# Attention weights exchanged between partition blocks before, instead of after, VectorE's block transposes

## The chip, the cores and the metric

The kernel runs on one core of one Trainium2 chip. A core has a TensorE (PE, with its weight loads listed apart as PEld), a VectorE (DVE), a ScalarE (ACT), a GpSimd (POOL) and a SyncE (SP) that here only issues DMAs; sixteen DMA engines move the data. [...] The metric is the device time of one execution, in microseconds; the median of three executions is given.

## The reference, cut to what matters

```python
# q, k, v: (8, 8, 576, 64) float32; tau a scalar
scores = scale * q @ k^T
thresh = max(scores) - tau
scores = where(scores >= thresh, scores, -1e9)
attn = softmax(scores)                    # exp, sum + 1e-9, divide
x = (attn @ v) as (4608, 512)
h = x @ w_in                              # (4608, 1024), weights float64
e = exp(h - max(h)); solu = h * e / (sum(e) + 1e-9)
ln = (solu - mean) / sqrt(var + 1e-6) * g_ln
out = ln @ w_out                          # (4608, 512)
```

The attention weights `attn` come out with the queries on the partitions. The product with `v` needs the keys on the partitions, so each block of weights has to be transposed.

## The kernel before, in words

**Rounds.** The attention is cut into 144 slots of two heads by 128 queries, 18 for each of the eight batches. A loop written out by hand (from L746) gives one round to each slot and puts the work of several slots and of the feed-forward part into every round, in a fixed order. In round s:

- PE makes the scores of slot s for two heads into two PSUM tiles `s_ps` (`scores`, L396). In some rounds it first turns q and k of a later batch (L269).
- DVE takes the negated row maxima (`maxes`, L412). ACT makes the threshold and a ramp, which is the first write of the weights `w` (`ramp`, L423 and L427), and then the exponentials in place with their sums `sm` (`exps`, L437). The ramp is the last reader of the score columns of `s_ps`; only then can PE write the scores of slot s+1.
- POOL normalises slot s-1: two small instructions make the reciprocal of the sums (L444, L445), and two of 128x576 multiply `w` in place (L447).
- DVE transposes the weights of slot s-1 in blocks of 32x32 (`blocks`, L459) into a tile `T` that serves two slots, a unit. After the second slot of a unit, SP issues four DMAs (L470) that take each 32 partitions of `T` and lay their two halves of columns out over 64 partitions of `wT`: 288 KB each, with runs of 4608 bytes.
- PE multiplies `wT` with `v` (`attend`, L495), for a unit whose second slot is s at round s+3 at the earliest.

**Feed-forward.** A tile of 128 tokens goes through rounds in a repeated pattern of four. In two rounds PE makes h (`ff_h`, L548), and in these two it also does one `attend` each. In the next two it makes the output of the tile before (`ff_o`, L650). I call them H1, H2, O1 and O2; H1 and H2 follow O2. In H2, DVE transposes the V of the tile before (`ff_turn`, L638) and takes the maximum of h (`ff_max`, L561), which ACT's exponential of h in round O1 needs (`ff_exp`, L570). In O1, DVE multiplies (`ff_mul`, L576) and POOL makes a reciprocal (`ff_sum`, L581). In O2, DVE makes mean and variance (L591, L592) and POOL five small results from them (`ff_stats`, L595 to L602). In H1, ACT and DVE normalise (L612, L617), and SP issues four DMAs that exchange halves of u with V (`ff_swap`, L628); the output of a tile is stored there too (L677). In the H1 round, a POOL memset (`fence`, L104) stands between PE's two parts of h.

**Order in a round.** The order in the program's loop is: loads of the next batch on SP, scores, maxes, ramps and exps, `normalise`, jobs of the middle (`ff_stats`; `ff_norm2` and `ff_swap`), PE's feed-forward and `attend`, `blocks`, late jobs (`ff_turn`, `ff_max`, `ff_mul`, `ff_sum`, `ff_store`). In the first 16 rounds each round ends with the conversion of one piece of the float64 weights on DVE and ACT (L221 to L247) and the DMAs of a later piece (L205, L210, L256).

**Buffers.** `w` has four buffers of one head each (two rounds), `T` and `wT` two each. All of the kernel's DMAs from round 0 on are issued by SP.

Of the kernel before, what the change touches and what calls it, by code (L numbers as in the profile page):

```python
# [8 lines left out]
F32 = mybir.dt.float32  # L9
# [4 lines left out]
ALU = mybir.AluOpType  # L14
AX = mybir.AxisListType
PSUM = bass.MemoryType.PSUM
P = 128
# [3 lines left out]
def kernel(  # L21
# [27 lines left out]
    nc = tc.nc  # L49
    B, H, S, D = q.shape  # L50
# [6 lines left out]
    NB = S // 32  # L57
    SCALE = 0.125
    ROWS = (slice(0, 64), slice(64, P))
# [4 lines left out]
    work = ctx.enter_context(tc.tile_pool(name="work", bufs=2))  # L64
# [21 lines left out]
    NK = S // 64  # L86
# [4 lines left out]
    units = {}  # L91
# [171 lines left out]
    def turn(spare, x, lhsT_of):  # L263

        o = spare["base"] + 64 * x
        to = slice(o, o + 64)
        for r in range(2):
            for y in range(2):
                nc.tensor.matmul(  # L269
                    out=spare[r][ROWS[y], to], lhsT=lhsT_of(r, y), rhs=ident[ROWS[r], ROWS[r]],  # L270
                    start=True, stop=True,
                )

    def seen(spare, r, x, n):
        o = spare["base"] + 64 * x
        return spare[r][:, o : o + 64 * n].rearrange("p (t k) -> p t k", t=n)

    def source(i):
        b, hp = divmod(i, NP)
        return halves[b, hp // 2], 2 * (hp % 2)  # L280

    def pair(i):
        if i not in pairs:
            pairs[i] = dict(
                qT=heads.tile([P, SM], F32, tag="qT", name="qT"),
                kT=heads.tile([P, S], F32, tag="kT", name="kT"),
                qe=heads.tile([P, ST], F32, tag="qe", name="qe"),
            )
        return pairs[i]
# [23 lines left out]
    def k_parts(i):  # L313

        return pair(i)["kT"].rearrange("p (c m k) -> p m c k", c=2, m=NK)

    def k_item(i, ts=slice(0, 4)):
        src, h0 = source(i)
        to = k_parts(i)
        n = ts.stop - ts.start  # L320

        def make(spare, x):
            for t in range(n):
                turn(spare, x + t, lambda r, y: src["k"][ROWS[r], h0 + y, ts.start + t])

        def keep(spare, x, r):
            (nc.vector.tensor_copy if r and not spare.get("eased") else nc.scalar.copy)(
                out=to[:, 4 * r + ts.start : 4 * r + ts.stop],
                in_=seen(spare, r, x, n).rearrange("p t (k c) -> p t c k", c=2),
            )  # L330

        return n, make, keep

    def e_item(i):
        src, h0 = source(i)
        last = k_parts(i)[:, NK - 1]

        def make(spare, x):
            turn(spare, x, lambda r, y: ends[i // NP][ROWS[r], 2 * (i % NP) + y])

        def keep(spare, x, r):
            if r == 0:
                nc.scalar.activation(
                    out=pair(i)["qe"], in_=seen(spare, 0, x, 1)[:, 0], func=AF.Copy, scale=scl
                )
            else:
                (nc.scalar.copy if spare.get("eased") else nc.vector.tensor_copy)(
                    out=last, in_=seen(spare, 1, x, 1)[:, 0].rearrange("p (k c) -> p c k", c=2)
                )

        return 1, make, keep
# [21 lines left out]
    live = {}  # L373
# [45 lines left out]
    def ramp(s, x):  # L419
        d = live[s]  # L420
        ps = d["ps"][x]
        nth = small.tile([P, 1], F32, tag="nth", name="nth")
        nc.scalar.activation(  # L423
            out=nth, in_=d["nth"][x], func=AF.Identity, bias=tau_t, scale=1.0
        )
        w = work.tile([P, S], F32, tag="w", bufs=4, name="w")
        nc.scalar.activation(  # L427
            out=w, in_=ps[:, 0:S], func=AF.Prelu, bias=nth, scale=1.0,
            alpha=1.0e30,
        )  # L430
        d.setdefault("w", []).append(w)

    def exps(s):
        d = live[s]
        d["sm"] = sm = small.tile([P, 2], F32, tag="sm", name="sm")
        for x, w in enumerate(d["w"]):
            nc.scalar.activation(  # L437
                out=w, in_=w, func=AF.Exp, bias=ntau, scale=1.0, accum_out=sm[:, x : x + 1]
            )

    def normalise(s):
        d = live[s]
        sm = d["sm"]
        nc.gpsimd.tensor_scalar(out=sm, in0=sm, scalar1=1e-9, scalar2=None, op0=ALU.add)  # L444
        nc.gpsimd.tensor_tensor(out=sm, in0=sm, in1=mone, op=ALU.pow)  # L445
        for x, w in enumerate(d["w"]):
            nc.gpsimd.tensor_scalar(  # L447
                out=w, in0=w, scalar1=sm[:, x : x + 1], scalar2=1.0, op0=ALU.mult, op1=ALU.mult
            )

    def blocks(s):
        b, kind, hp, r = slots[s]
        key = (b, kind, hp)
        if r == 0:
            units[key] = dict(T=work.tile([P, NB, 2, 2, 32], F32, tag="T", name="T"))
        u = units[key]
        T = u["T"]
        for h, w in enumerate(live.pop(s)["w"]):
            nc.vector.transpose(out=T[:, :, r, h, :], in_=w)  # L459
        if r == 0:  # L460
            return


        T = T.rearrange("p (c m) r h x -> p c (m r h x)", c=2)
        u["wT"] = wT = work.tile([P, 2, NK, 2, 2, 32], F32, tag="wT", bufs=2, name="wT")
        to = wT.rearrange("p g m r h x -> p g (m r h x)")
        for g in range(2):
            for half in range(2):
                of = 64 * half + 32 * g
                nc.sync.dma_start(out=to[ROWS[half], g], in_=T[of : of + 32])  # L470

# [234 lines left out]
    for b in range(1, B):  # L708
        r = PER * (b - 1)
# [7 lines left out]
    with tc.manual_schedule():  # L717
# [3 lines left out]
        for x in range(3):  # L721
# [4 lines left out]
            out=g_rows.rearrange("c (r g x) -> c r g x", r=2, g=2),  # L726
            in_=g_ln.rearrange("(g c r x) -> c r g x", g=2, r=2, x=32),
# [10 lines left out]
        rnd = 0  # L738
# [7 lines left out]
        while True:  # L746
# [29 lines left out]
            if more:  # L776
                room = SPARE
                if busy and quarter > 1 and preps and rnd + 4 < first_slot(preps[0][3]):
                    room = 0
                while preps and preps[0][0] <= rnd and preps[0][1] <= room:  # L780
                    _, n, make, _ = preps.pop(0)
                    items.append(make())
                    room -= n
                scores(rnd, items)
                maxes(rnd)
                ramp(rnd, 0)
                keeps(rnd, 0)
                keeps(rnd, 1)
                ramp(rnd, 1)
                exps(rnd)  # L790
            if rnd in whole:
                whole_pair(whole[rnd])
            if rnd - 1 in live:
                normalise(rnd - 1)
            for job in middle.pop(rnd, []):
                job()
            due = bool(pv_due) and pv_due[0][0] <= rnd
            step = None
            if quarter < 2 and cur is not None:
# [43 lines left out]
            if attending is not None:  # L843
# [4 lines left out]
                    ready.append((rnd + 1, [(b // 2,)]))  # L848
                elif kind < 2 and hp == NP - 1:
                    ready.append((rnd + 1, [(b, kind, 0), (b, kind, 1)]))  # L850
            if rnd - 1 in live:
                blocks(rnd - 1)
            for job in late.pop(rnd, []):
                job()
            if rnd == 2:
# [1 line left out]
            if rnd in pieces:  # L857
                x = pieces[rnd]
# [42 lines left out]
```

## Time and profile before

| | |
|---|---|
| median of three executions | 927.46 us (927.3 to 929.27) |
| the profiled execution | 931.87 us, of which the span from first to last instruction is 930.1 us |
| mean granted TensorE clock | 0.98 |
| busy: PE / DVE / ACT / POOL | 853.2 / 675.7 / 668.7 / 448.8 us |
| DMA queue of SP | 94472 packets, 150.13 MB, 70.0% of sixteen engines |
| `wT<-T` | 288 DMAs of 288 KB, median 5.8 us from issue to landing |
| `V<-u` | 144 DMAs of 64 KB, median 3.7 us from issue to landing |
| L447, the multiplications on POOL | 288 of 128x576, mean 768 ns |
| L459, the block transposes | 288 of 128x576, mean 750 ns |

In the profile's groups, a line gives: program line, engine, operation, tiles, shape and count, then the total and the mean duration, then the idle time just before these instructions and what ended it. A timeline's line gives: start, duration, engine, line, operation, tiles, shape, count, and in brackets the idle time ahead of it with what ended it; neighbouring instructions of one line are merged, so that the duration is that of all of them together. SPq stands for SP's instruction queue, where the duration is that of the issue and not of the transfer.

### The profile page before, as it was taken

The page shows a single profiled execution, that of the slowest core. Times are in us where ns is not written, and L with a number is a line of the kernel's source. Part 1 is how long each engine was busy: PE and PEld are TensorE (multiplying, and loading weights), DVE is VectorE, ACT ScalarE, POOL GpSimd, SP SyncE. Part 2 cuts the span into 40 slices and gives each one's busy share as a digit, 9 for nine tenths or more (in the row PEclk, how much of TensorE's full clock was granted, in tenths as well). Part 3 has the DMA queues.
Part 4 walks back from the last instruction along what each step waited for, and adds up shares of the span by engine and source line. Part 5 has one row for each costly group of instructions (what it writes and reads, how often), then busy time and mean ns, then how long its engine had stood idle before and what let it go on. Part 6 is the DMA issues. An engine that isn't in the chain of part 4 may idle for free. (4 is left out here: it accounts for less than half of the span.)

```text
span 930.1 us, 39744 instructions
## 1 busy us (share of the span) xinstructions
PE 853.2 (92%) x17089; PEld 643.3 (69%) x17089; DVE 675.7 (73%) x1015; ACT 668.7 (72%) x1531; POOL 448.8 (48%) x870
## 2 busy tenths in 40 slices
PE   4548689989999999989999999989998999999997
PEld 3325478857678778866677887767776877777555
DVE  4888977768767877767777777767876777787352
ACT  5767877878777877867777787868877777888121
POOL 1443555536545555545545555545555455655220
PEclk9978799999999999999999999999999999999999
DMA  8898967975879558965879467966889455866422
GB/s 245 195 224 229 223 162 187 229 176 126 182 163 226 128 129 191 238 137 128 189 166 227 108 134 185 230 147 132 189 180 211 114 130 127 185 145 139 96 47 47
DMA packets 95880, 154.63 MB, mean 166 GB/s; under 512 B 27608, under 2 KB 69592, under 8 KB 95704
## 3 DMA queue, kind: packets, MB, share of 16 engines
q1 hardware_dynamic: 94472, 150.13, 70.0%
q8 instruction: 134, 2.20, 1.0%
q10 hardware_dynamic: 1232, 1.97, 0.7%
q14 instruction: 42, 0.34, 0.1%
HBM read 46.14 MB, written 9.44 MB: 60 GB/s over the span
## 5 line engine op out<-in xcount | busy, mean ns | idle before, releaser
L412 DVE TENSOR_REDUCE nm<-s_ps 128x1 f32<-128x576 f32 x288 | 204.6, 752 | 164.5 <-PE s_ps L396 164.1
L650 PE MATMUL o_ps<-w,uT 64*64 64x256 f32 x4608 | 271.6, 378 | 7.5 <-DVE uT L638 4.6
L650 PEld LDWEIGHTS o_ps<-w,uT 64*64 64x64 f32 x4608 | 230.4, 134 | 56.5 <-issue 18.4
L427 ACT ACTIVATE w<-s_ps,nth 128x576 f32<-128x576 f32 x288 | 213.6, 742 | 20.2
L548 PE MATMUL h_ps<-w,xh 64*64 64x512 f32 x1856 | 222.5, 594 | 4.1 <-issue 4.1
L447 POOL TENSOR_SCALAR w<-w,sm 128x576 f32<-128x576 f32 x288 | 217.4, 768 | 14.4
L437 ACT ACTIVATE w<-w,ntau 128x576 f32<-128x576 f32 x288 | 219.1, 764 | 0.0
L459 DVE STREAM_TRANSPOSE T<-w 128x576 f32<-128x576 f32 x288 | 205.9, 750 | 6.1 <-POOL w L447 5.6
L495 PEld LDWEIGHTS pv<-wT,v 64*64 64x64 f32 x5760 | 169.5, 136 | 40.7 <-issue 28.1
L396 PE MATMUL s_ps<-kT,qT 64*64 64x512 f32 (+1 forms) x2048 | 174.8, 422 | 20.6 <-ACT w L427 17.9
L444 POOL TENSOR_SCALAR sm<-sm 128x2 f32<-128x2 f32 x144 | 36.7, 255 | 321.6 <-ACT w L437 318.9
L495 PE MATMUL pv<-wT,v 64*64 64x128 f32 (+1 forms) x5760 | 171.8, 263 | 11.3 <-DMA wT<-T 7.7
L548 PEld LDWEIGHTS h_ps<-w,xh 64*64 64x64 f32 x1856 | 116.0, 135 | 93.8 <-issue 71.0
L423 ACT ACTIVATE nth<-nm,tau_t 128x1 f32<-128x1 f32 x288 | 84.5, 294 | 95.6 <-DVE nm L412 95.2
L445 POOL TENSOR_TENSOR sm<-sm,mone 128x2 f32<-128x2 f32 x144 | 103.6, 719 | 12.0
L396 PEld LDWEIGHTS s_ps<-kT,qT 64*64 64x64 f32 x2048 | 66.0, 138 | 30.6 <-ACT w L427 25.7
L612 ACT ACTIVATE V<-u,nb,rs 128x1024 f32<-128x1024 f32 x36 | 44.6, 1240 | 32.3 <-POOL nb L602 32.3
L638 DVE STREAM_TRANSPOSE uT<-V 128x1024 f32<-128x1024 f32 x36 | 44.0, 1222 | 20.1 <-DMA V<-u 19.9
L517 ACT COPY xh<-pv 128x256 f32<-128x256 f32 x64 | 23.5, 367 | 44.7 <-PE pv L495 44.4
L437 ACT ACTIVATION_READ_ACCUMULATOR w<-w,ntau 128x1 f32 x288 | 54.7, 190 | 0.0
L570 ACT ACTIVATE u<-h_ps,hm 128x1024 f32<-128x1024 f32 x36 | 40.3, 1119 | 20.0 <-DVE hm L561 14.6
L561 DVE TENSOR_REDUCE hm<-h_ps 128x1 f32<-128x1024 f32 x36 | 43.0, 1194 | 11.6 <-PE h_ps L539 6.2
(74 smaller groups left out, 633.2 us busy)
## 6 DMA issues: line engine op xcount, KB each, us to landing
wT<-T SPq DMA_DIRECT2D x288, 288.0 KB, 5.8
V<-u SPq DMA_DIRECT2D x144, 64.0 KB, 3.7
out_dram<-ob SPq DMA_DIRECT2D x72, 128.0 KB, 2.8
v<-in_v_dram SPq DMA_DIRECT2D x16, 512.0 KB, 8.0
v<-in_v_dram SPq DMA_DIRECT2D x32, 256.0 KB, 7.4
q<-in_q_dram SPq DMA_DIRECT2D x15, 512.0 KB, 5.7
k<-in_k_dram SPq DMA_DIRECT2D x15, 512.0 KB, 7.7
raw<-in_moe_w_out_dram SPq DMA_DIRECT2D x32, 128.0 KB, 5.3
```

The costliest lines, as they stand in the source:

```text
L396: nc.tensor.matmul(out=ps[h][ROWS[y], ks], lhsT=lhsT, rhs=d["kT"][ROWS[h], ks], start=True, stop=True,)
L412: nc.vector.tensor_reduce(out=nm, in_=ps[:, 0:S], axis=AX.X, op=ALU.max, negate=True)
L423: nc.scalar.activation(out=nth, in_=d["nth"][x], func=AF.Identity, bias=tau_t, scale=1.0)
L427: nc.scalar.activation(out=w, in_=ps[:, 0:S], func=AF.Prelu, bias=nth, scale=1.0, alpha=1.0e30,)
L437: nc.scalar.activation(out=w, in_=w, func=AF.Exp, bias=ntau, scale=1.0, accum_out=sm[:, x : x + 1])
L445: nc.gpsimd.tensor_tensor(out=sm, in0=sm, in1=mone, op=ALU.pow)
L447: nc.gpsimd.tensor_scalar(out=w, in0=w, scalar1=sm[:, x : x + 1], scalar2=1.0, op0=ALU.mult, op1=ALU.mult)
L459: nc.vector.transpose(out=T[:, :, r, h, :], in_=w)
L495: nc.tensor.matmul(out=to, lhsT=d["v"][ROWS[u], h0 + h, m ^ 4 * u if m < 8 else m], rhs=rhs, start=m == 0, stop=m == NK - 1,)
L548: mm = nc.tensor.matmul(out=h[ROWS[y], f], lhsT=x[ROWS[r], c, ROWS[y]], rhs=w1[ROWS[r], c, f], start=part == 0 and c == 0, stop=part == 1 ...
L612: nc.scalar.activation(out=V, in_=u, func=AF.Identity, bias=nb, scale=rs)
L650: nc.tensor.matmul(out=d["o"][ROWS[z], 512 * r : 512 * r + 256], lhsT=d["uT"][ROWS[r], m].rearrange("p y x -> p (y x)"), rhs=w2[ROWS[r], m ...
```

## The change

The weights' columns of each head are exchanged between partition blocks before the transposes. `normalise` now writes a second tile `wx` instead of `w`, with the same product. A new step `spread`, after the jobs of the middle of the same round, lets POOL also multiply `w` in place, and then lets SP issue four DMAs for each slot: each takes half of the columns of both heads of 32 partitions from `w` into 32 other partitions of `wx`, 72 KB in runs of 1152 bytes. So half of each row of `wx` is POOL's, and half comes by DMA. `blocks` transposes `wx` straight into `wT`, two rounds after the slot instead of one; `T` and its DMAs are gone. `w` and `wx` have three buffers of two heads each. The columns of k are laid out in another order to fit (L329 and L348, source of a copy read in runs instead of every second element). The earliest round of `attend` is unchanged.

```diff
-                in_=seen(spare, r, x, n).rearrange("p t (k c) -> p t c k", c=2),
+                in_=seen(spare, r, x, n).rearrange("p t (c k) -> p t c k", c=2),
...
-        w = work.tile([P, S], F32, tag="w", bufs=4, name="w")
+        if x == 0:
+            d["w"] = work.tile([P, 2, S], F32, tag="w", bufs=3, name="w")
+        w = d["w"][:, x]
...
-        for x, w in enumerate(d["w"]):
+        d["wx"] = work.tile([P, 2, S], F32, tag="wx", bufs=3, name="wx")
+        times(d["wx"], d)
+
+    def times(to, d):
+        for x in range(2):
             nc.gpsimd.tensor_scalar(
-                out=w, in0=w, scalar1=sm[:, x : x + 1], scalar2=1.0, op0=ALU.mult, op1=ALU.mult
+                out=to[:, x], in0=d["w"][:, x], scalar1=d["sm"][:, x : x + 1], scalar2=1.0,
+                op0=ALU.mult, op1=ALU.mult,
             )
+    def spread(s):
+        d = live[s]
+        w, wx = d["w"], d["wx"]
+        times(w, d)
+        for g in range(2):
+            for half in range(2):
+                here, there = 64 * half + 32 * g, 64 * half + 32 * (1 - g)
+                nc.sync.dma_start(
+                    out=wx[here : here + 32, :, S // 2 * (1 - g) : S // 2 * (2 - g)],
+                    in_=w[there : there + 32, :, S // 2 * g : S // 2 * (g + 1)],
+                )
 
     def blocks(s):
...
-            units[key] = dict(T=work.tile([P, NB, 2, 2, 32], F32, tag="T", name="T"))
...
-        for g in range(2):
-            for half in range(2):
-                of = 64 * half + 32 * g
-                nc.sync.dma_start(out=to[ROWS[half], g], in_=T[of : of + 32])
+            units[key] = dict(
+                wT=work.tile([P, 2, NK, 2, 2, 32], F32, tag="wT", bufs=2, name="wT")
+            )
+        to = units[key]["wT"].rearrange("p g m r h x -> p (g m) r h x")
+        wx = live.pop(s)["wx"]
+        for h in range(2):
+            nc.vector.transpose(out=to[:, :, r, h, :], in_=wx[:, h])
...
             for job in middle.pop(rnd, []):
                 job()
+            if rnd - 1 in live:
+                spread(rnd - 1)
...
-            if rnd - 1 in live:
-                blocks(rnd - 1)
+            if rnd - 2 in live:
+                blocks(rnd - 2)
```

More of the change, by code (lines that the diff above doesn't have):

```diff
@@ L347, in keep @@
                 (nc.scalar.copy if spare.get("eased") else nc.vector.tensor_copy)(
-                    out=last, in_=seen(spare, 1, x, 1)[:, 0].rearrange("p (k c) -> p c k", c=2)
+                    out=last, in_=seen(spare, 1, x, 1)[:, 0].rearrange("p (c k) -> p c k", c=2)
                 )
@@ L430, in ramp @@
         )
-        d.setdefault("w", []).append(w)
     def exps(s):
@@ L435, in exps @@
         d["sm"] = sm = small.tile([P, 2], F32, tag="sm", name="sm")
-        for x, w in enumerate(d["w"]):
+        for x in range(2):
+            w = d["w"][:, x]
             nc.scalar.activation(
@@ L445, in normalise @@
         nc.gpsimd.tensor_tensor(out=sm, in0=sm, in1=mone, op=ALU.pow)
-        for x, w in enumerate(d["w"]):
+        d["wx"] = work.tile([P, 2, S], F32, tag="wx", bufs=3, name="wx")
+        times(d["wx"], d)
+    def times(to, d):
+        for x in range(2):
             nc.gpsimd.tensor_scalar(
-                out=w, in0=w, scalar1=sm[:, x : x + 1], scalar2=1.0, op0=ALU.mult, op1=ALU.mult
-            )
+                out=to[:, x], in0=d["w"][:, x], scalar1=d["sm"][:, x : x + 1], scalar2=1.0,
+                op0=ALU.mult, op1=ALU.mult,
+            )
+    def spread(s):
[9 more added lines that the diff above has]
+                )
     def blocks(s):
@@ L454, in blocks @@
         if r == 0:
-            units[key] = dict(T=work.tile([P, NB, 2, 2, 32], F32, tag="T", name="T"))
[L456 to L466, printed above, removed]
-        for g in range(2):
-            for half in range(2):
-                of = 64 * half + 32 * g
-                nc.sync.dma_start(out=to[ROWS[half], g], in_=T[of : of + 32])
+            units[key] = dict(
[5 more added lines that the diff above has]
+            nc.vector.transpose(out=to[:, :, r, h, :], in_=wx[:, h])
     def attend(key):
```

## The prediction

> **What bounds the kernel now.** I read the page's busy shares and slices first.
>
> ```profile
> PE 853.2 (92%) x17089; PEld 643.3 (69%) x17089; DVE 675.7 (73%) x1015; ACT 668.7 (72%) x1531; POOL 448.8 (48%) x870
> PE   4548689989999999989999999989998999999997
> DMA  8898967975879558965879467966889455866422
> ```
>
> There are two stages. In the first six slices (140 us) PE is half busy and the DMA engines are full. After that PE is full, so only what makes PE wait can cost time there. The waits show what the change could relieve:
>
> ```profile
> PE pv L495 <- DMA wT<-T: 7.7, 2, 7.3
> DVE T L459 <- POOL w L447: 5.6, 7, 3.3
> ```
>
> PE waited twice for the DMA that goes (7.7 us in all, one of them 7.3 us long, in the first 70 us). The next view is the timeline of one four-round cycle in the full stage: PE, DVE, POOL and ACT around 430 us.
>
> ```profile
> 425.08 1.18 PE L396 MATMUL s_ps<-kT,qT 64*64 64x64 f32 x16
> 426.05 3.66 PE L650 MATMUL o_ps<-w,uT 64*64 64x256 f32 x64
> 429.50 1.18 PE L396 MATMUL s_ps<-kT,qe 64*64 64x64 f32 x16
> ```
> ```profile
> 421.64 1.43 DVE L459 STREAM_TRANSPOSE T<-w 128x576 f32<-128x576 f32 x2
> 422.99 1.20 DVE L638 STREAM_TRANSPOSE uT<-V 128x1024 f32<-128x1024 f32 x1
> 424.12 1.18 DVE L561 TENSOR_REDUCE hm<-h_ps 128x1 f32<-128x1024 f32 x1
> 426.35 1.42 DVE L412 TENSOR_REDUCE nm<-s_ps 128x1 f32<-128x576 f32 x2 [1.05 <-PE s_ps L396]
> ```
> ```profile
> 430.87 0.23 POOL L444 TENSOR_SCALAR sm<-sm 128x2 f32<-128x2 f32 x1 [2.51 <-ACT w L437]
> 432.00 1.48 POOL L447 TENSOR_SCALAR w<-w,sm 128x576 f32<-128x576 f32 x2
> 433.68 0.34 POOL L595 TENSOR_SCALAR rs<-mv,se 128x1 f32<-128x1 f32 x1 [0.20 <-DVE mv L592]
> 435.72 0.23 POOL L444 TENSOR_SCALAR sm<-sm 128x2 f32<-128x2 f32 x1
> ```
> ```profile
> 425.61 1.12 ACT L570 ACTIVATE u<-h_ps,hm 128x1024 f32<-128x1024 f32 x1
> 427.15 0.30 ACT L423 ACTIVATE nth<-nm,tau_t 128x1 f32<-128x1 f32 x1 [0.32 <-DVE nm L412]
> 428.53 0.74 ACT L427 ACTIVATE w<-s_ps,nth 128x576 f32<-128x576 f32 x1
> ```
>
> Round O1 begins on PE at 425.08 and O2 at 429.50. From PE's own starts a whole cycle is 22.66 us (6.96 H1, 6.84 H2, 4.42 O1, 4.43 O2), with no gap. But the reserve is small: the ramp that frees `s_ps` ends at 429.27 and PE wants it at 429.50. Ahead of it ACT had 0.32 us idle, and DVE 1.05 us.
>
> Last, the price of a DMA without traffic, from the end of the chain that ended last:
>
> ```profile
> 912.71 0.57 SPq L628
> 913.34 0.58 SPq L628
> 914.60 2.02 DMA V<-u
> ```
>
> Issues follow at 0.63 us, and the last of four lands 2.02 us after its issue began.
>
> [...] halving bytes need not shorten an issue, and V<-u (64 KB, median 592 ns) against wT<-T (288 KB, median 625 ns) agrees. [...] The transposes show no such thing (1.42 us a pair beside POOL or not), so I charge nothing for more POOL work beside them.
>
> **The change part by part.**
>
> *Bytes.* 288 x 288 KB = 83 MB go, 576 x 72 KB = 41 MB come. In the full stage this alone is worth nothing, because PE doesn't wait for DMA there. In the first stage it removes at most the 7.3 us wait and a 3.8 us wait of DVE for weights: -11 us. The copy of k in another order: zero, same count and size.
>
> *SP.* Per two slots, eight issues instead of four. At 0.63 us that is 5.0 against 3.6 us in the profile (it issues wT<-T at 0.9 us under load). SP has room on average (2.5 us in each round of 5.7, and some 5 us a cycle of V<-u and stores), but each queue position now counts.
>
> *POOL.* 288 more multiplications of 0.74 us: +213 us, 448.8 to 662 us, 71% of the span. No bound on average: a cycle has 4 x (1.13 + 1.55 + 1.55) + 3.0 = 19.9 us of 22.66. But in O2 and H1 the work is in one piece.
>
> *The wait.* DVE's transposes no longer follow POOL's product, they follow four DMAs that follow a second product. Behind them in DVE's queue stand, in H2, uT (L638), the maximum of h (L561) and the next scores' maxima (L412); ACT's exponential and ramps wait for these, and PE's next scores wait for the ramp. I walk through the cycle from O2's begin of POOL, 430.87 (slot of O1):
> - product into `wx`: 1.13 + 1.55, to 433.55; the five small ones begin at 433.68 as now and take 2.04, to 435.72; product in `w` 1.55, to 437.27.
> - SP issues spread of O1's slot, four times 0.63, to 439.79. V<-u could go at 438.85 (now 416.22 + 22.66) but stands behind it: to 442.31.
> - POOL, slot of O2: 1.13 + 1.55 + 1.55, to 441.50. The fence memset follows it at about 441.6 instead of 439.2; PE's second part of h begins at 442.3, so it is just covered, by 0.7 us.
> - SP issues the spread of O2's slot only at 442.31; its last issue begins at 444.20, lands 2.02 later, and DVE sees it at 446.29.
> - The transposes stood at 421.64 + 22.66 = 444.30: 2.0 us late. Then 1.35 + 1.13 + 1.18, the maximum of h at 449.95; ACT's exponential 0.08 + 1.10; thresholds and ramps 2.12 (427.15 to 429.27): 453.25. PE would want it by 452.16 and gets it at 453.35: 1.2 us late.
> - The exponentials of that slot end 1.60 later, so POOL begins the next cycle at 454.85, 23.98 after 430.87.
>
> The last line matters: the chain closes on itself, so 24.0 us is a bound for every cycle, 1.3 us over PE's 22.66. In H1 the same walk makes the transposes 2.4 us late (441.1 for 438.77), which DVE's idle 2.37 us just hold. In O1 and O2 they land about when they are due.
>
> How many cycles? I took the starts of L412 in every fourth round of the trace: 31 cycles from round 16 on, from 21.6 us (the last batch, no q and k to prepare) to 27.8 us. 24 of them are shorter than 24.0, and together they lack 36 us. The longer ones hide the chain.
>
> *The unknowns.* Issue of a 72 KB DMA: between 0.56 us (shortest V<-u, 507 ns, with the 0.05 gap) and 0.75 (V<-u under traffic, 3.04 us for four); I take 0.63, eleven of them lie in the chain. Landing: 2.02 to 3.7 us (median V<-u); I take 2.02, since the 288 KB transfers that delayed V<-u are gone. At the lower end the cycle is 23.2 us (sum +18), and POOL's own path (441.50 instead of 442.31) would hold it there; at 0.75 with a landing of 2.0 it is 25.3, and the sum about +65.
>
> *Loads.* q, k and v stand in SP's queue in four rounds of a batch, two to five issues of 0.6 to 0.75 us, and can't be put beside the spread. Most find SP idle (O2), some stand ahead of a spread that has 1 us of reserve. I take 1.2 us in each of seven batches: +8 us (0 to 20).
>
> *The first stage.* DVE is nearly full there: a round of 5.4 us is maxima, transposes and 2.56 us of weight conversion. Over three rounds the new chain is POOL 4.2, SP and landing, then DVE 1.35 + 2.56 + 0.75, ACT 3.7: 12.6 us plus DMA. Idle engines give 1.9 + 2.0 (5.5 us a round, no loss); the present 0.9 us an issue and 5.8 us landing give 2.7 + 5.8 (7.0 a round, +1.6 for 14 rounds, +23). Fewer bytes draw it to the lower half: I take +14 for half a dozen late rounds and more, less 9 of the 11 us of relief: +5 (-11 to +20).
>
> Sum: 36 + 8 + 5 = 49 us. Against the profiled execution, 931.9 + 49 = 981. That one lies 4.4 us over the median of the runs shown, so for a median: 976 us.
>
> **The rivals.** *Queues worse than idle ones (slower still).* SP issues at 0.75 us and lands later, because loads and spreads share it: +65, with loads +12 and first stage +10: about 1015. For it: four V<-u issues took 3.04 us in O2/H1 now. Against: that was behind 288 KB transfers. *Covered (near zero).* The chain is at its lower end, 23.2 us, loads find idle time and the start gains 8: +18 - 8 = 10, about 937; with the chain below 22.66, no change. For it: the DMA wait is 2 us against a 1.4 us reserve, so little decides. *Faster.* The start is the one place where PE waited for these bytes: the relief of 11 us remains whole, 916 us. It decides if an issue takes 0.51 us or less with POOL's path shorter by 0.5 us too, so that the cycle stays at PE's 22.66. Against: no issue of V<-u shorter than 507 ns plus its gap is in the trace. That the change doesn't do what it says is not open: the built order of the instructions has the four DMAs ahead of each pair of transposes, on which these wait, and no other new wait of DVE.
>
> **How the numbers follow.** Forecast (950 to 1000) 0.62; worse queues 0.18; covered 0.12, a third of it within 0.2%; faster 0.08. 0.2% is about what a measurement of this kernel can tell from no change. So faster 0.08, same 0.04, slower 0.88. The range reaches down to the covered case's 937 and up to 1012, just short of the worse one's centre, which leaves out the faster and half of the worst.
>
> **What would show it.** In the changed profile: DVE's L482 waits for the DMA wx<-w, about 2 us in H1 and in H2, as the largest new wait; PE's L396 waits for ACT's ramp in each O2 round, about 1.3 us; PE's busy share falls to about 88%; cycles in the full stage of 24 us; POOL near 660 us busy at an unchanged 740 ns; DMA share near half. I am wrong if the cycles stay at 22.7 us (then the DMAs land before DVE comes), if the first stage moves by over 15 us either way, or if POOL's or SP's own queue grows from cycle to cycle.

## The result and the profile after

| | before | after |
|---|---|---|
| median of four executions on one chip | 928.37 us (927.3 to 933.67) | 1041.85 us (1040.14 to 1044.71) |
| the profiled execution, and its span | 931.87 us, 930.1 us | 1042.83 us, 1041.1 us |
| mean granted TensorE clock | 0.980 | 0.943 |
| start, to the maxima of round 17 | 124.4 us | 135.9 us |
| full stage, from there to those of round 143 | 729.8 us | 826.0 us |
| rest | 75.9 us | 79.1 us |

The changed kernel is slower: the ratio is 1.121, with a 95% interval of 1.116 to 1.126. The last three rows cut the two spans at the same instructions (L412 of round 17 and of the last slot). Of the 111 us, 11.5 come in the start, 96.2 in the full stage and 3.2 at the end.

The page of the changed kernel, first busy times and slices, then SP's DMA queue:

```profile
PE 893.6 (86%) x17089; PEld 631.5 (61%) x17089; DVE 671.6 (65%) x1015; ACT 667.1 (64%) x1531; POOL 669.7 (64%) x1158
...
PE   4557777888998998889988998899989999899997
...
DMA  8666533733445324542446234542347322422221
...
q1 hardware_dynamic: 117512, 107.68, 41.4%
```

DMA is relieved (70.0% of the engines' time before), DVE and ACT did what they did, and POOL has its 221 us more. None of them is full, and PE, with the same 17089 matmuls, now stands at 7 to 9 tenths where it had been at 9. So it waits. The waits of the changed kernel (engine and instruction, what ended the wait, then total us, times, longest):

```profile
DVE wT L482 <- DMA wx<-w: 225.9, 77, 6.7
...
ACT nth L423 <- DVE nm L412: 136.8, 83, 6.8
...
ACT u L582 <- DVE hm L573: 93.7, 30, 6.3
...
PE s_ps L396 <- ACT w L429: 47.5, 50, 5.3
PE o_ps L662 <- DVE uT L650: 46.9, 29, 4.8
...
PE pv L507 <- DVE wT L482: 2.9, 2, 2.6
```

The same waits in the kernel before, where the transposes waited 5.6 us, for POOL:

```profile
ACT nth L423 <- DVE nm L412: 95.2, 104, 2.5
...
PE s_ps L396 <- ACT w L427: 17.9, 14, 3.0
...
ACT u L570 <- DVE hm L561: 14.6, 7, 5.1
...
PE o_ps L650 <- DVE uT L638: 4.6, 3, 2.5
```

The last line of the changed kernel is the one to read first. PE hardly ever waits for the transposed weights themselves. It waits for what stands behind the transposes in DVE's order: uT directly, and the maximum of h and the scores' maxima by way of ACT's ramp. PE's waits for uT grew from 4.6 to 46.9 us, and its waits for the ramp before the scores from 17.9 to 47.5. One cycle shows it. DVE, PE and SP of the changed kernel:

```profile
525.63 1.44 DVE L482 STREAM_TRANSPOSE wT<-wx 128x576 f32<-128x576 f32 x2 [4.85 <-DMA wx<-w]
526.99 1.38 DVE L412 TENSOR_REDUCE nm<-s_ps 128x1 f32<-128x576 f32 x2
531.08 1.44 DVE L482 STREAM_TRANSPOSE wT<-wx 128x576 f32<-128x576 f32 x2 [2.70 <-DMA wx<-w]
532.44 1.20 DVE L650 STREAM_TRANSPOSE uT<-V 128x1024 f32<-128x1024 f32 x1
533.57 1.18 DVE L573 TENSOR_REDUCE hm<-h_ps 128x1 f32<-128x1024 f32 x1
```
```profile
530.20 1.16 PE L396 MATMUL s_ps<-kT,qT 64*64 64x64 f32 x16
533.79 3.68 PE L662 MATMUL o_ps<-w,uT 64*64 64x256 f32 x64 [2.44 <-DVE uT L650]
537.26 0.31 PE L396 MATMUL s_ps<-kT,qT 64*64 64x64 f32 x4
538.00 1.19 PE L396 MATMUL s_ps<-kT,qT 64*64 64x64 f32 x12 [0.43 <-ACT w L429]
```
```profile
520.12 2.58 SPq L467 DMA_DIRECT2D wx<-w  x4
522.80 3.24 SPq L640 DMA_DIRECT2D V<-u  x4
526.14 2.58 SPq L467 DMA_DIRECT2D wx<-w  x4
```

DVE stands idle for 4.85 us in H1 and 2.70 us in H2 for the exchange; uT and the maximum of h begin when the second wait is over, and PE's output starts 2.44 us late. (The last of the four `V<-u` was issued at 525.46 and landed 1.97 us later, at 527.43: what kept uT until 532.44 was its place in DVE's order.) The three series on SP follow each other almost without a gap: SP could have begun the third when POOL was done, at 524.65, and began at 526.14 because V<-u stood ahead of it. POOL began this cycle at 514.13 and the next at 539.55: 25.42 us.

### The profile page after: what moved, and what is told of

It is laid out like the page before. It is cut to its first block, busy times and chain, and to the rows that moved or that the text cites. A ratio compares the mean times of both kernels' runs of the same rounds, so it can differ in the third digit from the quotient of the medians.

```text
span 1041.1 us, 40957 instructions
## 1 busy us (share of the span) xinstructions
PE 893.6 (86%) x17089; PEld 631.5 (61%) x17089; DVE 671.6 (65%) x1015; ACT 667.1 (64%) x1531; POOL 669.7 (64%) x1158
## 3 DMA queue, kind: packets, MB, share of 16 engines
q10 hardware_dynamic: 1232, 1.97, 0.6%
## 5 line engine op out<-in xcount | busy, mean ns | idle before, releaser
L482 DVE STREAM_TRANSPOSE wT<-wx 128x576 f32<-128x576 f32 x288 | 206.6, 755 | 264.5 <-DMA wx<-w 225.9
L662 PE MATMUL o_ps<-w,uT 64*64 64x256 f32 x4608 | 276.6, 389 | 47.5 <-DVE uT L650 46.9
L662 PEld LDWEIGHTS o_ps<-w,uT 64*64 64x64 f32 x4608 | 224.2, 138 | 118.4 <-issue 87.0
L412 DVE TENSOR_REDUCE nm<-s_ps 128x1 f32<-128x576 f32 x288 | 203.0, 745 | 50.8 <-PE s_ps L396 50.7
L453 POOL TENSOR_SCALAR wx<-w,sm 128x576 f32<-128x576 f32 x288 | 215.5, 760 | 14.3
L396 PE MATMUL s_ps<-kT,qT 64*64 64x64 f32 (+1 forms) x2048 | 181.6, 436 | 49.8 <-ACT w L429 44.6
L507 PEld LDWEIGHTS pv<-wT,v 64*64 64x64 f32 x5760 | 166.0, 138 | 38.5 <-issue 25.8
L507 PE MATMUL pv<-wT,v 64*64 64x128 f32 (+1 forms) x5760 | 168.3, 265 | 5.2 <-DVE wT L482 2.9
L560 PEld LDWEIGHTS h_ps<-w,xh 64*64 64x64 f32 x1856 | 108.8, 138 | 103.1 <-issue 90.5
L447 POOL TENSOR_TENSOR sm<-sm,mone 128x2 f32<-128x2 f32 x144 | 111.3, 773 | 12.0
L588 DVE TENSOR_TENSOR u<-h_ps,u 128x1024 f32<-128x1024 f32 x36 | 42.8, 1189 | 8.5 <-ACT u L582 8.5
```

The source lines that it names most:

```text
L396: nc.tensor.matmul(out=ps[h][ROWS[y], ks], lhsT=lhsT, rhs=d["kT"][ROWS[h], ks], start=True, stop=True,)
L412: nc.vector.tensor_reduce(out=nm, in_=ps[:, 0:S], axis=AX.X, op=ALU.max, negate=True)
L453: nc.gpsimd.tensor_scalar(out=to[:, x], in0=d["w"][:, x], scalar1=d["sm"][:, x : x + 1], scalar2=1.0, op0=ALU.mult, op1=ALU.mult,)
L482: nc.vector.transpose(out=to[:, :, r, h, :], in_=wx[:, h])
L507: nc.tensor.matmul(out=to, lhsT=d["v"][ROWS[u], h0 + h, m ^ 4 * u if m < 8 else m], rhs=rhs, start=m == 0, stop=m == NK - 1,)
L560: mm = nc.tensor.matmul(out=h[ROWS[y], f], lhsT=x[ROWS[r], c, ROWS[y]], rhs=w1[ROWS[r], c, f], start=part == 0 and c == 0, stop=part == 1 ...
```

## The experiments

My theory (A in the expectations): the transposes stand in DVE's order at the end of a long chain, POOL's two products, SP's issues and the landing, and this chain closes on itself; what counts is what stands behind the transposes. Rivals: B, POOL's doubled work costs by itself, in its order or by contention; C, SP's queue is what is too full; D, loads of q, k and v would cost any version as much. The kernel before ran beside each experiment, and a ratio is against it; its medians lay between 927.9 and 930.8 us, so a few microseconds between two experiments say nothing.

**1. Transposes behind the next round's maxima (e1_later_blocks).** They go from the end of a round to the next round, behind its maxima and ahead of the jobs of the middle.

```diff
                 normalise(rnd - 1)
+            if rnd - 3 in live:
+                blocks(rnd - 3)
             for job in middle.pop(rnd, []):
...
-            if rnd - 2 in live:
-                blocks(rnd - 2)
```

> The changed kernel with only the place of VectorE's transposes moved: not at the end of the round two after the slot, but in the round three after it, just behind that round's maxima and copies. Same POOL work, same DMAs, same issues. Theory A (the transposes wait in VectorE's order for DMAs that stand at the end of a long chain, POOL twice, SP, landing, and the chain closes on itself): 3 us and more of reserve open the chain, cycles fall to 22.7 to 23.2 us, the time to 925 to 955 us, VectorE's wait for wx<-w under 50 us. Theory B (GpSimd's doubled work itself, by its length or by contention with VectorE): unchanged, 1010 to 1045. Theory C (SP's queue is full with twice as many issues): 990 or more, the wait moves to PE's product with v.

Measured: 982.59 us (973.47 to 985.03), ratio 1.055 (1.044 to 1.066). The same DMAs, the same POOL work: 59 us less than the changed kernel. That is less than A's 925 to 955 asked for, and below B's and C's figures. The waits of this kernel:

```profile
POOL rs L607 <- DVE mv L604: 88.2, 36, 6.8
ACT V L624 <- POOL nb L614: 76.9, 36, 5.0
...
DVE wT L482 <- DMA wx<-w: 34.5, 14, 5.2
```

The wait for the exchange fell from 225.9 to 34.5 us. But my edit made a new one: mean and variance in O2 are a job of the middle, and now stand behind the transposes; POOL's five small results wait 88.2 us for them (43.7 in the changed kernel).

**2. The spread ahead of the jobs of the middle (e2_spread_ahead).**

```diff
                 normalise(rnd - 1)
+                spread(rnd - 1)
             for job in middle.pop(rnd, []):
                 job()
-            if rnd - 1 in live:
-                spread(rnd - 1)
```

> The changed kernel with the step that multiplies w and issues the four DMAs put ahead of the middle jobs: in O2 ahead of GpSimd's five small instructions, in H1 ahead of V<-u in SP's queue. Same work. Theory A: the spread of O2's slot no longer stands behind V<-u, so it lands 2 us earlier; but V<-u now stands behind it, lands later, and the transposes of V wait for that: the chain to the maximum of h gains only 0.3 to 1.1 us a cycle, 1005 to 1035 us, and a new wait of uT for V<-u. If SP's order at that place is the whole cause: below 985.

Measured: 1039.7 us (1035.58 to 1040.95), ratio 1.119 (1.114 to 1.124): no gain over the changed kernel, and just above what I expected. Its waits:

```profile
DVE wT L482 <- DMA wx<-w: 110.4, 62, 6.7
...
ACT V L624 <- POOL nb L614: 57.9, 36, 5.0
...
DVE uT L650 <- DMA V<-u: 42.2, 27, 2.8
```

The largest wait was halved, and nothing was won: uT now waits 42.2 us for V<-u (5.0 before the edit), which had become the later one on POOL and SP. Here the job pulled ahead pushed another back by as much.

**3. Half of the exchange's DMAs (e3_half_the_dmas).** One half of the columns isn't exchanged, so half of the moved weights are missing from the result; POOL's work and all waits remain.

```diff
-            for half in range(2):
+            for half in range(1):
```

> The changed kernel without two of the four DMAs of each slot: half of the exchange of weights between partition blocks is left out. GpSimd's work is unchanged. Theory A: eight of the issues in the chain become four, 2.6 us less in a cycle, and less in front of loads; cycles near PE's 22.7 to 23.3, time 940 to 975 us. Theory B: 1030 to 1045. Theory C: like A, but with a gain of half of the doubled issues, about 980.

Measured: 959.88 us (956.39 to 970.02), ratio 1.035 (1.025 to 1.044). POOL's busy time is unchanged at 668.8 us, and 82 of the 113.5 us between the medians are gone with 288 of SP's 576 issues and their bytes, inside A's 940 to 975. So most of the loss depends on SP's and the landings' part of the chain. What is left, some 30 us, isn't POOL's alone: the transposes still wait 133.5 us for the DMAs that remain.

**4. The kernel before with a second product on POOL (e4_before_twice_pool).** A multiplication by one follows each normalisation, so the transposes and the five small results come later by its 1.5 us a slot; no DMA is added.

```diff
+        for x, w in enumerate(d["w"]):
+            nc.gpsimd.tensor_scalar(
+                out=w, in0=w, scalar1=mone[:, 0:1], scalar2=-1.0, op0=ALU.mult, op1=ALU.mult
+            )
```

> The kernel before with GpSimd's doubled work and nothing else of the change: after the normalisation it multiplies the same weights once more, by one, in place; the transposes wait for that. Theory A: only 1.5 us more ahead of the transposes against reserves of about 1 us, 0 to 1 us a cycle: 928 to 960 us. Theory B: most of the loss, 1000 us and more. Theory C: 928, no wait of PE.

Measured: 969.31 us (963.83 to 973.53), ratio 1.043 (1.035 to 1.051), between A's figures and B's.

```profile
DVE T L463 <- POOL w L451: 125.3, 105, 3.2
```

The transposes, which had waited seven times for POOL, now wait 105 times; 1.5 us is more than the reserve in most rounds.

**5. The same without the transposes behind it (e9_before_pool_aside).** POOL multiplies into a scratch tile that nothing reads, at the place of the spread. Four products of 128x256 took 478 ns each (median), so 1.9 us a slot instead of the 1.5 that I meant to add. (A small constant tile shares a buffer to make room.)

```diff
+    def again(s):
+        ...
+        for x, w in enumerate(d["w"]):
+            for c in range(2):
+                nc.gpsimd.tensor_scalar(
+                    out=more, in0=w[:, 256 * c : 256 * c + 256], scalar1=sm[:, x : x + 1],
+                    scalar2=1.0, op0=ALU.mult, op1=ALU.mult,
+                )
...
+            if rnd - 1 in live:
+                again(rnd - 1)
```

> The kernel before with four more GpSimd products of 128x256 for each slot, at the place in GpSimd's order where the changed kernel has its second product, into a scratch tile that nobody reads: GpSimd's doubled work without anything that waits for it except GpSimd's own queue. Theory A: 928 to 942 us (the fence and the next normalisation a little later). Theory B (contention or length of GpSimd's work as such): 955 to 975, as with the product in place ahead of the transposes (969).

Measured: 953.28 us (948.91 to 958.34), ratio 1.028 (1.020 to 1.035).

```profile
DVE T L470 <- POOL w L447: 96.8, 70, 3.3
...
PE h_ps L559 <- POOL mark L104: 23.8, 29, 1.8
```

Nothing waits for the added products, and still they cost 25 us: the fence memset, queued behind them, holds PE for 23.8 us, and the real products of the next slot come later. The time lies between A's 928 to 942 us and B's 955 to 975, nearer to B's. This is B's cost in order. Contention I don't find: L447 itself takes 751 ns on average here, 768 in the kernel before, and DVE's busy time is 678.1 us here and 671.6 in the changed kernel, where it was 675.7.

**6. No loads after batch 1, with its control (e5_after_no_loads, e6_before_no_loads).** Batches 2 to 7 use the q, k and v of batch 1 again; the first is the changed kernel, the second the kernel before with the same edit.

```diff
     def load_qk(b, hf):
+        if b > 1:
+            halves[b, hf] = dict(halves[1, hf])
+            ends[b] = ends[1]
+            return
...
     def load_v(b, hf):
+        if b > 1:
+            halves[b, hf]["v"] = halves[1, hf]["v"]
+            return
```

> The changed kernel with the loads of q, k and v of the batches 2 to 7 left out (they compute with batch 1's). Theory A with loads as a large term that I priced at 8 us (issues ahead of the spread's in SP's queue, slower landing): cycles of 27 to 32 us go, all are 24.3 to 25.5, time 990 to 1015 us. If the loads are as small as I priced them: 1030 to 1040, and long cycles stay. Theory B: 1035 to 1045.

> The kernel before with the loads of q, k and v of the batches 2 to 7 left out (they compute with batch 1's); the control to the same edit on the changed kernel, which took 40 us off. Theory A (loads cost the changed kernel because its spreads stand behind them in SP's queue): the kernel before gains less, 5 to 20 us (its wait for V<-u), 908 to 924 us. Theory D (loads cost any version the same): 35 to 45 us, 885 to 895.

Measured: 1001.18 us (1000.53 to 1005.96), ratio 1.079 (1.071 to 1.086), and for the control 914.62 us (913.64 to 918.19), ratio 0.986 (0.981 to 0.991). Loads cost the changed kernel 40.7 us and the kernel before 13.3 us, so D is wrong by 27 us. The pair also gives the chain without loads: the full stage is 786.7 us against 716.3, that is +70.4 us. The cycles, taken from the starts of the maxima (L412, here L419) in every fourth round, have a median of 24.8 us against 22.65 us. The time is inside the first figure expected, but not all cycles are: the longest takes 29.1 us.

**7. Mean and variance ahead of the transposes, fence on DVE (e7_later_and_fence).** Experiment 1 with its new wait mended, and the memset taken off POOL.

```diff
-        m = nc.gpsimd.memset(mark, 0.0)
+        m = nc.vector.memset(mark, 0.0)
...
+            for job in first.pop(rnd, []):
+                job()
+            if rnd - 3 in live:
+                blocks(rnd - 3)
...
-                middle.setdefault(rnd + 2, []).append(lambda t=cur: ff_stats(t))
+                first.setdefault(rnd + 2, []).append(lambda t=cur: ff_stats(t))
```

> The run with later transposes, and two more edits: the fence's memset on VectorE instead of behind GpSimd's products, and in round O2 mean and variance ahead of the transposes. Theory A (what is left in its clean cycles of 23.3 us is GpSimd's one piece of work in O2 and H1, in front of the fence): clean cycles 22.7 us, 30 x 0.6 us less than 982: 955 to 970 us; the wait of PE for mark is gone. Theory B (contention with GpSimd's doubled work): 975 to 990.

Measured: 941.22 us (939.75 to 942.89), ratio 1.014 (1.009 to 1.019): 101 of the 113.5 us between the two kernels are gone, more than A's 955 to 970 asked for, with the same DMAs and POOL busy for 670.6 us.

```profile
ACT V L624 <- POOL nb L614: 30.2, 27, 5.0
...
ACT w L429 <- DMA wx<-w: 20.9, 11, 4.6
...
POOL rs L607 <- DVE mv L604: 16.8, 31, 2.2
```

The two waits of experiment 1 are small again. One that came with the later transposes (30.6 us in experiment 1) is left: eleven ramps wait for a buffer of `w` that the exchange still reads.

**8. The fence alone (e12_later_fence_only).** Experiment 1 with the memset on DVE only, to part the two edits of experiment 7.

```diff
-        m = nc.gpsimd.memset(mark, 0.0)
+        m = nc.vector.memset(mark, 0.0)
```

> The run with later transposes (982 us) with only the fence's memset on VectorE; mean and variance stay behind the transposes in O2. Between 982 and 941. If the fence alone was what GpSimd's long piece held: near 945. If the later start of the five small instructions (1.4 us behind the transposes) was the rest: near 960, with V<-u late and uT waiting for it.

Measured: 978.83 us (975.98 to 980.26), ratio 1.054 (1.049 to 1.059): 4 us less than experiment 1, inside the spread of that one's runs. It lies between 941 and 982 as expected, but above both figures named (945 and 960). So the order of mean and variance is the larger edit, 38 us on top of the fence. That order with the fence left on POOL wasn't tried.

**9. Loads on ACT's queue (e8_loads_on_act).** From batch 1 on, ACT issues the loads in place of SP.

```diff
-                queue = nc.scalar if nm == "k" and x + 1 < len(parts) else nc.sync
+                queue = nc.scalar if b > 0 or nm == "k" and x + 1 < len(parts) else nc.sync
...
-            nc.sync.dma_start(
+            (nc.scalar if b > 0 else nc.sync).dma_start(
```

> The changed kernel with the loads of q, k and v from batch 1 on issued by ScalarE's queue instead of SP's. Same bytes. If the loads cost by standing ahead of the spreads in SP's queue and rings: most of the 40 us come back, 1000 to 1018 us, less what ScalarE's issues cost (16 of about 0.6 us a batch). If they cost through the DMA engines that they fill: 1030 to 1045, or slower where ScalarE waits for a buffer.

Measured: 1089.77 us (1088.58 to 1100.79), ratio 1.177 (1.169 to 1.185): slower than anything else. The issues of the loads don't start at once, and now hold up ACT's own work (ahead of one threshold five of them start between 440.37 and 446.71, and ACT stands idle for 12.8 us):

```profile
ACT nth L423 <- DMA v<-in_v_dram: 47.3, 5, 12.8
```

That swamps whatever SP won, so this run doesn't tell why loads cost the changed kernel more.

**10. Loads dealt out, with its control (e10_later_fence_split, e11_before_split).** Experiment 7, and the kernel before, with the loads of a batch spread over more rounds, mostly one DMA or two in each (q and k of each half get rounds of their own, and so do the parts of the first half of v; four of the second half's five stay together, in lines that aren't shown).

```diff
+        for at, hf in zip((2, 7) if b > 1 else (6, 10), range(2)):
+            for i in range(2):
+                load_at.setdefault(r + at + i, []).append(
+                    lambda b=b, hf=hf, i=i: load_qk(b, hf, (i,))
+                )
+        for i, which in enumerate(((0,), (1,), (2,), (3, 4))):
+            load_at.setdefault(r + (9 if b > 1 else 14) + i, []).append(
+                lambda b=b, which=which: load_v(b, 0, which)
+            )
```

> The 941 us version with the loads of q, k and v dealt out over single rounds, one or two DMAs each, instead of up to five in one. Its long cycles (25 to 27.8 us, where a ramp or a transpose waits for DMAs stuck behind loads, 20 and 16 us in all) should lose half of their excess: 920 to 933 us, at or under the kernel before. If loads cost by their total and not by coming together: 938 to 944.

> The kernel before with the loads dealt out in the same way, as control: it can gain at most the 13 us that leaving out the loads gave; 918 to 928 us.

Measured: 932.27 us (924.88 to 937.05), ratio 1.0022 (0.9999 to 1.0045), and for the control 932.45 us (926.88 to 937.43), ratio 1.0022 (1.0000 to 1.0044). Another 9 us are gone, as expected; the control won nothing, where 918 to 928 us was expected. This is the best version with the exchange ahead of the transposes, and it is level with the kernel before, with every part of the change in it, the new order of k's columns included. No version that does the whole work beat that one.

## Why the prediction was wrong

The direction and most of the mechanism were right: the transposes wait for wx<-w in H1 and H2, uT, the maximum of h and the next maxima come late behind them, ACT's ramps after these, POOL is busy for 669.7 us (662 forecast), and DMA's share fell to 41% (near half forecast). One path to PE was not in it: PE's output takes uT directly. By the walk's own figures uT ends at 448.77 (446.29 + 1.35 + 1.13), just when PE's output is due (426.05 + 22.66 = 448.71), so all further lateness went straight to PE; 46.9 us of its waits end with uT. The size was wrong, 111 us in the spans where 49 were forecast. By the terms of the sum:

| term | forecast | measured |
|---|---|---|
| start | +5 | +11.5 |
| chain in the full stage | +36 | +70.4 (experiment 6, without loads) |
| loads | +8 | +26 (96.2 less 70.4) |
| end | 0 | +3.2 |

The start's loss goes with the same repairs as the chain's: in experiment 7 the start takes 124.5 us again. Three readings of the prediction are slightly off and move nothing: 416.22 + 22.66 is 438.88 (not 438.85), H1's landing by the walk is 441.25 (not 441.1), and the shortest cycle from round 16 on is 21.2 us (not 21.6).

**"I take 0.63, eleven of them lie in the chain", and "I take 2.02" for the landing.** This is the step that failed first. Both came from four lone DMAs at the end of the program. Up to SP the walk holds: POOL's second product for O1's slot ended at 520.10 (forecast, moved to this cycle by 83.26 us: 520.53), its work for O2's slot at 524.65 (524.76). Then V<-u took 3.24 us in place of 2.52, the last issue of the spread began 0.6 us later than forecast, and DVE went on 3.0 us after it began in place of 2.1. The next cycle began 1.44 us late by that, at 25.42 us instead of 23.98. The view of the exchange's source line says why an unloaded DMA is the wrong measure. First for the whole run (shortest, median and longest issue in ns; the same of the landing in us), then for the four DMAs of this cycle's last series:

```profile
L467 SPq DMA_DIRECT2D wx<-w x576: 585/596/1824, 23.4 to 975.6; - x192
...
DMA to landing us min/median/max: 2.0/2.1/6.6
```
```profile
DMA to landing us min/median/max: 2.8/3.3/3.8
```

The exchange's medians are as good as the forecast's; the tails aren't, and a closed chain meets them nearly every time. Of the 980 DMA issues in the changed kernel, 71 took over 1 us, and 70 of these 71 followed another issue within 0.2 us, as those of the chain do. The full stage has 26 cycles in which the three series stand directly behind each other in SP's queue: 22 of them have such an issue among the eleven; the cycle shown had one of 1.37 us in V<-u. On average of the 26, the last issue begins 7.98 us after the first (forecast: 11 x 0.63 = 6.93), and DVE goes on 2.50 us later (forecast: 2.09). Without loads (experiment 6) the figures are 8.01 and 2.41 us over 30 cycles: 1.4 us above the forecast in all, which would make 25.4 us out of 23.98; the cycles there average 25.1. The prediction had seen 3.04 us for V<-u before and blamed the 288 KB transfers; with these gone, the median series of four still takes 3.09 us.

**"The longer ones hide the chain."** Over experiment 6's control, lifting each of 31 cycles to 24.0 us costs 41 us, to the measured median of 24.8 about 63; the rest up to 70 is in cycles that were longer than the chain and got longer still. My reading, which no run tests alone, is that a long cycle doesn't start from rest: its chain is late already. In the changed kernel, loads included, the cycles average 26.4 us and reach 32.6, where the longest before was 27.8.

**"1.2 us in each of seven batches: +8 us."** Loads cost 26. It isn't slower issuing: without them 68 of 884 issues took over 1 us, with them 71 of 980. The loss lies where the loads are: the 20 cycles of the changed kernel with a load's issue in them average 27.1 us, the 11 without 24.9 (23.6 and 22.6 in the kernel before). That it is their standing ahead of the exchange in SP's queue is made likely only for the repaired order, where dealing them out took 9 us away. For the changed kernel itself, how they cost so much stays open, since experiment 9 failed to tell.

**PE's own speed** was not priced at all. Of the 111 us, 40.4 are PE's busy time for the same matmuls, 70.6 its idle time. PE in the changed kernel, and the granted clock (third number from the end) in the stretches around it:

```profile
450.20 1.24 PE L396 MATMUL s_ps<-kT,qT 64*64 64x64 f32 x15
456.20 6.15 PE L662 MATMUL o_ps<-w,uT 64*64 64x256 f32 x64 [4.75 <-DVE uT L650]
462.16 1.16 PE L396 MATMUL s_ps<-kT,qT 64*64 64x64 f32 x16
463.13 3.64 PE L662 MATMUL o_ps<-w,uT 64*64 64x256 f32 x64
```
```profile
456.00:463.00 7.00, 6.80 (x80) 4.43 (x84) 4.94 (x7) 4.57 (x10) 1.75 (x4) 0.63 0.26 66
463.00:467.00 4.00, 4.00 (x97) 2.94 (x93) 3.62 (x7) 2.74 (x7) 2.04 (x4) 1.00 0.00 0
```

After a wait of 4.75 us the same 64 matmuls took 6.15 us, at a granted clock of 0.63 over the stretch (0.59 over the 6.15 us alone), instead of 3.64 us at 1.00. Shorter waits were followed by the same, but not always: after 2.36 and 2.70 us (at 747.20 and 774.17) the same matmuls took 5.37 us at a clock of 0.68, after the 2.44 us of the cycle above 3.68 us at 1.00. So three of these four waits were followed by slower matmuls, a further loss of 1.7 to 2.5 us each. Over the full stage the mean clock was 0.97 against 1.00 and PE's busy time 33 us longer. Three per cent of 707 us are 21; I have not broken down the rest, nor how much of it other waits hid. With the waits gone it goes too: PE is busy for 856.4 us in experiment 10.

**The rivals.** "Queues worse than idle ones" at 1015 us came nearest, for reasons given against it too lightly; it was 27 us too low, about half of that in the loads (+12 there, +26 measured). "Covered" would have been possible with a better order: experiment 10, at +0.2%, is that case. B is right in one part: POOL's doubled work costs 25 to 40 us by its place in POOL's order alone (experiments 4 and 5), where the prediction charged nothing and trusted 0.7 us of reserve at the fence; contention had no part in it that I could see (the transposes took 750 ns on average before, 755 in the changed kernel, POOL's products 768 and 763). In the changed kernel itself the fence cost little (PE's weight loads waited 6.4 us for it), and experiment 10 has the doubled work at +0.2%. C isn't right as a bound: half of the issues and bytes took 82 us of the loss with them (experiment 3), but in experiment 10 all of them are there, and the time is level with the kernel before.

## What to carry to other kernels

When a step is put behind a DMA, look first at what is queued behind that step on its engine: here the transposed weights were in time (PE waited 2.9 us for them), and the loss came from three instructions that stood behind the transposes and had no part in the exchange. If the new wait closes a loop over several queues, price it by the typical series under traffic, tail included, not by a lone DMA without traffic (here 10.5 us from the first issue until DVE goes on, where the lone DMA's prices gave 9.0), and don't let long cycles "hide" it (the longest grew from 27.8 to 32.6 us). A move to a later place then gives much of the loss back (59 of 113 us), but check what the moved step itself now stands ahead of (38 us more).

## What the runs showed of the hardware beyond that

- About one in fourteen of the DMA issues took 1.0 to 2.0 us where the median is 0.60 (71 of 980 in the changed kernel, 68 of 884 without loads; 190 of 692 over 1 us in the kernel before, with its 288 KB transfers). Nearly all of the slow ones stand behind another: of the 98 issues in SP's queue of the changed kernel that came first or after a pause of 0.2 us or more, one was slow, of the other 877, 70. For 72 KB an issue took 0.60 us against 2.1 us to landing (medians), and four in a row, at 2.58 us, took longer than the landing.
- Of four exchange DMAs in a row, in the full stage of the changed kernel, the last landed 2.1 us after its issue began in the median, and after 2.7 us or more in a quarter of the series (28 of 109).
- A POOL product of 128x256 with bfloat16 output took 478 ns (median, experiment 5), one of 128x576 in float32 749 ns (median, kernel before): less than half the elements at nearly two thirds of the time.
